# A hand-planned attention and MoE kernel: the same steps in another order, on other engines and in other buffers

## The chip, the cores and the metric

The kernel runs on one core of one Trainium2 chip. A core has five engines that run side by side, each from its own queue in the order in which the instructions were written: TensorE (PE in the profile, with its weight loads as PEld), VectorE (DVE), ScalarE (ACT), GpSimd (POOL) and SyncE (SP), which here mainly issues transfers. Sixteen DMA engines move the data. The metric is the time of one execution on the device in microseconds (us), lower is better.

## The reference

Four batches of eight heads, 768 positions of 64 numbers. Each position attends to itself and the 95 positions before it, and to the first 8 positions; a bias grows with the distance. The result, 3072 tokens of 512 numbers, goes through two matrix products with a SoLU and a layer norm between them.

```python
scores = scale * np.matmul(q, k.transpose(0, 1, 3, 2))
...
bias = -slopes[:, None, None] * dist[None, :, :]
scores = np.where(keep, scores + bias[None], -1000000000.0)
a = np.exp(scores - np.max(scores, axis=-1, keepdims=True))
a = a / (np.sum(a, axis=-1, keepdims=True) + 1e-09)
x = np.matmul(a, v)                    # to (B*S, H*D) by token
...
h = x @ w_in
e = np.exp(h - np.max(h, axis=-1, keepdims=True))
solu = h * e / (np.sum(e, axis=-1, keepdims=True) + 1e-09)
ln = (solu - mu) / np.sqrt(var + 1e-06) * g_ln
out = ln @ w_out
```

## The kernel before

The program is written in two passes. In the first, the function builds a list of 1094 *steps* by calls of `step`; each has a number (the count of the calls), the engines on which it may run, the buffers that it takes and a function that emits its instructions. In the second, `Plan.order` walks three written lists: ORDER gives the numbers of the steps in the order in which they are emitted, SLOTS the buffer of each pool that a step takes, ENGS the engine of each step that has a choice (casts, copies, factor products, squares, statistics, the issue of the last stores). Since each engine works in the order of emission, these lists are the whole schedule. Waits between engines are put in from the data and buffers that the instructions share. A fourth list, WARM, names places (position in ORDER, PSUM bank, count) at which filler matmuls on a constant tile are emitted, so that PE is busy while it would wait (L1233).

What the steps do, with the names used below:

- Loads. SyncE issues q and k by batch and pair of heads (four pairs, p0 to p3; L475 and L482), v by pair in two halves (L489), v's end rows (`vends`, L497) and its first 8 rows (`vglob`, L504), the four quarters of w_in (L615), of w_out (L625), and g (L578). From the ninth transfer on, each issue also waits until an earlier one has landed.
- Casts to 16 bits of x (q or k; `x32` to `x16`), of v and of w_in (`copy`, L264 on ACT, L266 on DVE, L268 on POOL). q and k are then turned: by PE (`turn_q`, `turn_k`, L735) and copied out of PSUM, except in batch 3, where a transfer turns them (L770).
- Attention, by batch: `scores` in two groups of six blocks for each pair (bias by PE in batch 0, L872; products L886), the exponential on ACT (L894), and in batches 1 to 3 a multiplication by the factor `fb` (`fac`, L903, DVE or POOL). The first 8 positions have their own small keys (`kg`, L521, POOL), `gscores` (L940, L946) and values (`vgz`, L513, POOL). By unit of 384 queries (unit 0 and unit 1): `sums` (L967, L976), their logarithm and split, `spread` (L1022), A·V in two parts (`av1`, `av2`, L1066 and L1056), and the product xT (L1091, DVE). A·V needs all casts of v of that batch that it reads, the end rows among them.
- The MoE part, by tile of 128 tokens (24 tiles, t0 to t23): `gemm1` (eight matmuls, L1125), `ef` (ACT, L1131), `u` (DVE, L1134), the sum of squares `sq` (ACT L1141 or DVE L1145), then u is turned, in tiles 0 to 4 by PE (`turn_u`, L1160), from tile 5 on by a transfer (`uturn`, L1150; four `uu` buffers hold u, six places of `late` the turned one), `gemm2` (L1206), scaling (`osb`, L1217 or L1220) and the store (L1224).
- Once: w_out is scaled by g in eight blocks (`gw`, L638, L641, L645), its `mean` is taken by PE (L652), and the blocks are centred (`centre`, L656, DVE). gemm2 needs that.
- The statistics of each group of three tiles (`stats`, L1180 to L1183) and the scale from them (L1187, L1189).

PSUM has eight banks, taken one at a time or two at a time (`big`, by scores and gemm1).

Of the kernel before, what the change touches and what calls it, by code (L numbers as in the profile page):

```python
# [29 lines left out]
FACT = {1, 2, 3}  # L30
SPLIT = False
ORDER = """
# [28 lines left out]
"""  # L61
SLOTS = """
# [10 lines left out]
"""  # L73
ENGS = """
# [4 lines left out]
"""  # L79
WARM = """  # L80
25:0:16 30:2:4 37:3:2 48:5:3 59:3:2 117:7:4 156:6:5
"""


# [1187 lines left out]
```

## Time and profile before

| what | us |
| --- | --- |
| median of 3 runs (154.2 to 154.55) | 154.37 |
| the profiled execution | 154.43 |
| its span, first to last instruction | 152.7 |
| PE, ACT, DVE, POOL busy in it | 144.4, 123.3, 116.7, 67.2 |
| PE filler matmuls (36) | 10.8 |

The engine rows of the profile give the busy time of each engine; a busy PE is not PE at its peak. A row of a timeline gives the start, the length, the engine with its line, the operation, the tiles written and read, and in brackets how long the engine stood idle before it and what ended that. SPq rows are SyncE issuing transfers.

### The profile page before, as it was taken

Reading aid. Unit: us, or ns where it says so; the run is one execution under the profiler, and the core shown is the slowest. Engines: PE = TensorE matmul, PEld = TensorE weight load, DVE = VectorE, ACT = ScalarE, POOL = GpSimd, SP = SyncE. Lnnn points to the kernel's source line nnn. Section 1 sums busy time; section 2 is a strip of 40 time slices with the busy share of each in tenths; the row PEclk is TensorE's granted clock in tenths of the full one; section 3 lists DMA queues with packets and bytes.
Section 4 is the critical chain, followed back from the end, with each engine's and each line's share of the span. In section 5 each row is a group of like instructions: output and inputs, shape, how many; then the busy total and the mean of one; then the engine's idle time right before and its main releaser. Section 6 shows DMA issues by size and latency. Waiting matters only on the chain.

```text
span 152.7 us, 4815 instructions
## 1 busy us (share of the span) xinstructions
PE 144.4 (95%) x1877; PEld 77.6 (51%) x1877; DVE 116.7 (76%) x241; ACT 123.3 (81%) x212; POOL 67.2 (44%) x188
## 2 busy tenths in 40 slices
PE   6979799999999999999999999989999999999991
PEld 2445557467655466744454645444445644444450
DVE  6729978799999997889899857289794884898200
ACT  3948999699999989899997896796875776884642
POOL 7675446548399849935921233755031000110000
PEclk9999999999999999999999999999999999999999
DMA  4999999999999899999999999998999975488743
GB/s 133 372 298 341 288 380 336 355 339 397 282 272 189 235 300 234 229 266 253 237 131 228 249 167 236 177 206 171 197 216 228 197 214 112 88 227 219 228 158 137
DMA packets 76431, 36.35 MB, mean 238 GB/s; under 512 B 65457, under 2 KB 71929, under 8 KB 76409
## 3 DMA queue, kind: packets, MB, share of 16 engines
q1 hardware_dynamic: 76120, 35.54, 96.3%
q10 hardware_dynamic: 288, 0.52, 0.9%
q8 instruction: 14, 0.23, 0.7%
q14 instruction: 9, 0.07, 0.1%
HBM read 23.15 MB, written 6.29 MB: 193 GB/s over the span
## 4 chain that ended last, share of the span: by engine, by line
PE 67%; DMA 8%; SPq 7%; DVE 7%; ACT 5%; issue 3%; POOL 0%; DVEq 0%; ACTq 0%
PE acc L1206 22%; PE acc L1125 21%; PE acc L1066 7%; DMA x<-in_q_dram 3%; SPq L489 3%; DMA late<-uu 3%; PE acc L735 3%; PE acc L886 3%; PE acc L967 3%; PE acc L1022 2%; DMA v<-in_v_dram 2%; DVE uu L1134 2%; ACT ef L1131 2%; SPq L475 1%; PE acc L1056 1%
## 5 line engine op out<-in xcount | busy, mean ns | idle before, releaser
L1125 PE MATMUL acc<-w_in_sb,xT 128*128 128x512 f16 x192 | 44.4, 379 | 0.0
L1206 PE MATMUL acc<-gw_out_sb,late 128*128 128x512 f16 (+1 forms) x200 | 44.3, 371 | 0.0
L1134 DVE SCALAR_TENSOR_TENSOR uu<-ef,acc 128x1024 f16<-128x1024 f16 x24 | 29.2, 1217 | 6.4 <-ACT ef L1131 5.7
L894 ACT ACTIVATE eb<-acc 128x896 f16<-128x896 f32 (+1 forms) x32 | 29.3, 962 | 2.0 <-PE acc L886 2.0
L1131 ACT ACTIVATE ef<-acc 128x1024 f16<-128x1024 f32 x24 | 24.8, 1035 | 5.9 <-PE acc L1125 5.9
L1206 PEld LDWEIGHTS <-late 128*128 128x128 f16 x200 | 18.9, 98 | 20.9 <-issue 0.7
L1125 PEld LDWEIGHTS <-xT 128*128 128x128 f16 x192 | 18.1, 98 | 21.4 <-issue 1.1
L268 POOL CAST x<-x 128x384 f16<-128x384 f32 (+1 forms) x32 | 19.0, 622 | 20.3 <-DMA x<-in_q_dram 6.1
L1091 DVE TENSOR_TENSOR xT<-acc,rr 128x384 f16<-128x384 f32 x32 | 16.4, 551 | 4.4 <-ACT rr L1031 2.9
L1066 PE MATMUL acc<-eb,v 64*64 64x160 f16 (+4 forms) x448 | 16.0, 221 | 0.6 <-POOL v L268 0.3
L1141 ACT ACTIVATE sqa<-uu 128x1024 f16<-128x1024 f16 x15 | 16.1, 1071 | 0.0
L1066 PEld LDWEIGHTS <-v 64*64 64x64 f16 x448 | 12.7, 106 | 4.5 <-issue 2.7
L1031 ACT ACTIVATE rr<-acc 128x768 f32<-128x768 f32 x16 | 12.6, 811 | 2.2 <-PE acc L1022 1.3
L903 DVE TENSOR_TENSOR eb<-eb,fb 128x896 f16<-128x896 f16 (+1 forms) x19 | 13.0, 710 | 0.9 <-ACT eb L894 0.9
L903 POOL TENSOR_TENSOR eb<-eb,fb 128x240 f16<-128x240 f16 (+1 forms) x20 | 12.8, 670 | 0.2 <-ACT eb L894 0.2
L268 POOL CAST v<-v 128x384 f16<-128x384 f32 (+3 forms) x21 | 9.7, 476 | 7.1 <-DMA v<-in_v_dram 7.0
L735 PE MATMUL acc<-ident,x 128*128 128x128 f16 x144 | 11.1, 220 | 1.2 <-ACT x L264 0.7
L1233 PE MATMUL acc<-busy 128*128 128x512 f16 x36 | 10.8, 439 | 1.5 <-DVE busy L550 1.5
L886 PE MATMUL acc<-qT,kT 64*64 64x160 f16 (+2 forms) x384 | 11.3, 227 | 0.3 <-ACT qT L264 0.3
L1145 DVE SCALAR_TENSOR_TENSOR sqv<-uu 128x1024 f16<-128x1024 f16 x9 | 11.0, 1219 | 0.1
L735 PEld LDWEIGHTS <-x 128*128 128x128 f16 x144 | 8.4, 98 | 4.9 <-ACT x L264 1.9
L1217 ACT ACTIVATE x<-acc,rstd 128x512 f32<-128x512 f32 (+1 forms) x9 | 5.8, 640 | 6.2 <-PE acc L1206 6.2
(120 smaller groups left out, 206.2 us busy)
## 6 DMA issues: line engine op xcount, KB each, us to landing
x<-in_q_dram SPq DMA_DIRECT2D x16, 384.0 KB, 5.9
x<-in_k_dram SPq DMA_DIRECT2D x16, 384.0 KB, 5.3
out_dram<-osb SPq DMA_DIRECT2D x12, 256.0 KB, 4.8
v<-in_v_dram SPq DMA_DIRECT2D x12, 192.0 KB, 4.8
out_dram<-x SPq DMA_DIRECT2D x9, 256.0 KB, 2.2
late<-in_moe_w_in_dram SPq DMA_DIRECT2D x4, 512.0 KB, 6.6
w_out<-in_moe_w_out_dram SPq DMA_DIRECT2D x4, 512.0 KB, 6.0
v<-in_v_dram SPq DMA_DIRECT2D x12, 160.0 KB, 4.4
```

The source lines that it names most:

```text
L268: nc.gpsimd.tensor_copy(out=out, in_=in_)
L735: nc.tensor.transpose(out=pt[:, ts(j, P)], in_=a[:, j, ts(pp, P)], identity=ident)
L886: nc.tensor.matmul(out=sc[o : o + 64, par, col : col + n], lhsT=kk[r, BLK * c : BLK * c + BLK], rhs=qq[r, g0 : g0 + n], start=fresh, stop= ...
L894: ex["fn"] = (lambda ex=ex, qk=qk, gw=gw: nc.scalar.activation(out=eb[at(qk, "eb")][:, :, 0:gw], in_=big(qk)[:, :, 0:gw], func=AF.Exp, sca ...
L903: (nc.gpsimd if fx["at"] == "POOL" else nc.vector).tensor_tensor(out=e[:, :, y], in0=e[:, :, y], in1=fb[:, p, :, y], op=ALU.mult)
L1066: nc.tensor.matmul(out=o_[64 * h : 64 * h + 64, gl : gl + m], lhsT=vv[r, v_at(vi, h, c), pair, :], rhs=view(eb[at(e_own[b, gi, pair], "eb" ...
L1091: nc.vector.tensor_tensor(out=xT[at(xt_own[b], "xT")][:, p, q0:q1], in0=one(av, d)[:, 0:w], in1=rr[at(re, "rr")][:, d, 0:w], op=ALU.mult)
L1125: nc.tensor.matmul(out=ph()[:, ts(fh, 512)], lhsT=xT[at(xt_own[b], "xT")][:, j, ts(t % NA, P)], rhs=w_in_sb[:, j, ts(fh, 512)], start=(j = ...
L1131: ex["fn"] = lambda g1=g1, t=t, ph=ph: nc.scalar.activation(out=ef[at(g1, "ef")], in_=ph(), func=AF.Exp, accum_out=s0[:, t : t + 1])
L1134: u["fn"] = lambda u=u, g1=g1, t=t, ph=ph: nc.vector.scalar_tensor_tensor(out=uu[at(u, "uu")], in0=ef[at(g1, "ef")], scalar=USC, in1=ph(), ...
L1141: nc.scalar.activation(out=sqs_["ACT"], in_=uu[at(u, "uu")], func=AF.Square, scale=float(D_FF) ** 0.5, accum_out=s2[:, t : t + 1])
L1206: nc.tensor.matmul(out=one(g2)[:, 0:wd], lhsT=uT[at(el_o, "uT")][:, c, :], rhs=gw_out_sb[:, c, sl_], start=(c == 0), stop=(c == NFC - 1))
```

## The change

The four lists are replaced. No step is added, removed or cut differently, and no other line is touched. ORDER names the same 736 steps; of those behind the first eight transfers all orders are free.

```diff
 ORDER = """
-126 86 12 11 271 2 13 17 16 10 15 66 14 18 0 20 73 36 3 75 7 1 4 88 68 69 89 22 53 55 56 90 8 70 38 79 81
...
+126 271 24 52 6 12 2 13 16 60 15 11 3 4 18 5 20 86 66 0 68 23 62 73 99 36 14 17 53 19 22 88 89 7 75 76 90
...
 SLOTS = """
-0 1 2 3 4 5 0 0 1 2 0 0 1 1 2 0 0 1 3 3 1 2 4 2 2 3 4 0 5 1 2 5 6 3 0 0 1 3 3 1 2 1 0 2 2 3 3 1 1 4 2 2 0
...
+4 0 2 1 3 5 1 0 6 5 0 1 4 0 1 3 2 1 2 4 6 3 0 5 6 2 2 1 3 4 3 3 1 2 4 2 1 3 2 1 0 0 3 0 2 11 3 0 2 0 1 1
...
 ENGS = """
-1 0 0 1 1 1 1 1 2 0 2 1 0 0 2 0 1 0 1 0 0 0 1 2 2 2 1 1 2 0 0 1 1 1 1 0 1 2 2 0 2 1 2 1 0 1 0 0 1 1 1 0 1
...
+1 1 2 1 0 0 2 1 1 1 1 0 0 1 1 0 1 0 1 0 0 0 1 2 2 1 0 0 1 0 0 2 0 2 2 0 2 2 1 0 0 0 2 0 1 0 1 2 1 1 0 0 0
...
 WARM = """
-25:0:16 30:2:4 37:3:2 48:5:3 59:3:2 117:7:4 156:6:5
+9:0:4 24:0:16 59:0:2 80:4:4 117:6:5 166:3:2
```

Read out by engine, the lists say this:

| place | before | after |
| --- | --- | --- |
| first transfers on SyncE | q2 k1 q1 vglob k0 vglob k2 vends (batch 0) | g q0 q2 k1 q1 q3 vglob k0 (batch 0) |
| last quarter of w_in, of w_out (place in SyncE's line) | 28th, 45th | 28th, 45th |
| first matmul steps behind the first fillers | turn_k p1, turn_q p2 | turn_q p2, turn_q p1 |
| fillers | 16, 4, 2, 3, 2, 4, 5 | 4, 16, 2, 4, 5, 2 |
| right ahead of the first gemm1 (t2) | 5 fillers | turn_k of batch 1, p1 |
| behind the mean, not ahead of it | | gscores of batch 1 unit 1, scores of batch 1 group 0 p2 |
| uturn of t6, t7 in SyncE's line | 101st, 103rd | 95th, 98th |
| v loads of batch 3 in SyncE's line | 83rd, 89th, 110th to 115th | 103rd, 107th, 109th to 116th (with a uturn and a store between) |
| turning of batch 3's q and k by SyncE | 86th to 108th | 82nd to 106th |
| ends of PE's line | gemm2 t22, t21, t13, t23 | gemm2 t18, t16, t22, t21, t23 |

POOL's line between the last block of w_out and the cast of the end rows of batch 1 reads, before: kg, kg, cast k (batch 2, p1), fac, fac, cast v, cast q (batch 2, p1), stats, cast v, cast of the end rows; behind it vgz and a cast of v. After: kg, kg, cast v, kg, cast k (batch 2, p1), fac, cast q (p0), cast k (p0), cast q (p1), stats, fac (batch 1, group 1, p2), vgz, cast v, cast v, cast of the end rows.

Engines of the steps that have a choice, before and after:

| step | before | after |
| --- | --- | --- |
| cast of k | POOL 10, DVE 2, ACT 4 | POOL 9, DVE 4, ACT 3 |
| cast of q | POOL 7, DVE 6, ACT 3 | POOL 12, DVE 4 |
| cast of v, of its end rows | POOL 12 + 2, DVE 4 + 2, ACT 4 | POOL 15 + 3, DVE 1 + 1, ACT 4 |
| copy of turned k, q from PSUM | ACT 8 + 5, DVE 4 + 7 | ACT 7 + 9, DVE 5 + 3 |
| cast of w_in | POOL 4, ACT 2, DVE 2 | POOL 2, ACT 2, DVE 4 |
| gw | DVE 5, POOL 2, ACT 1 | POOL 5, ACT 2, DVE 1 |
| fac | DVE 19, POOL 5 | DVE 16, POOL 8 |
| sq | ACT 15, DVE 9 | ACT 12, DVE 12 |
| stats | POOL 6, DVE 2 | POOL 3, DVE 5 |
| osb | ACT 15, DVE 10 | ACT 17, DVE 8 |
| tripling of the bias | DVE | POOL |
| issue of the last stores | SP 3, ACT 2 | SP 4, ACT 1 |

79 rows, old and new, of tables (ENGS, ORDER, SLOTS) are left out of this document.

## The prediction

> **What bounds the kernel now.** First the page's engine table and its slices, then the sums by stage over five stretches that I chose at the places where the work changes its kind.
>
> ```profile
> PE 144.4 (95%) x1877; PEld 77.6 (51%) x1877; DVE 116.7 (76%) x241; ACT 123.3 (81%) x212; POOL 67.2 (44%) x188
> ...
> PE   6979799999999999999999999989999999999991
> ```
> ```profile
> 0.00:27.00 27.00, 23.41 (x380) 13.42 (x381) 19.81 (x60) 22.04 (x34) 16.18 (x75) 1.00 1.00 307
> 27.00:43.00 16.00, 15.35 (x242) 9.59 (x244) 14.88 (x30) 14.74 (x27) 9.38 (x20) 1.00 1.06 339
> 43.00:95.00 52.00, 52.00 (x755) 28.23 (x758) 46.21 (x84) 47.88 (x85) 31.62 (x68) 1.00 1.12 230
> 95.00:117.00 22.00, 21.11 (x264) 10.00 (x253) 16.04 (x28) 17.19 (x28) 9.20 (x22) 1.00 1.02 198
> 117.00:150.00 33.00, 32.55 (x260) 16.37 (x256) 19.81 (x42) 21.39 (x41) 0.83 (x4) 1.00 0.72 182
> ```
>
> In the sums the columns are busy us of PE, PEld, DVE, ACT and POOL, then the granted clock, the DMA share and GB/s. TensorE is the bound: from 43 to 95 us it is busy 52.00 of 52.00. What an order of the same steps can win is PE's idle time alone, because the matmuls stay: 3.59 us before 27 us (and the fillers there), 0.65 us from 27 to 43, 0.89 us from 95 to 117. The 0.45 us of the last stretch lie behind the last matmul. The first two stretches are paced by transfers: DMA shares of 1.00 and 1.06 mean that the engines' queues are full.
>
> **The change part by part.** No instruction's work changes except by its engine, so I take it place by place. I read ORDER engine by engine and ask at each place which matmuls stand ahead of it.
>
> *The start, up to the first gemm1 (tile 2).* In both orders exactly the same matmul steps stand ahead of it, and SyncE issues the same 28 transfers up to the last quarter of w_in. This is what happens there now:
>
> ```profile
> 26.14 1.24 PE L1233 MATMUL acc<-busy 128*128 128x512 f16 x5
> ...
> 27.22 1.89 PE L1125 MATMUL acc<-w_in_sb,xT 128*128 128x512 f16 x8
> ```
> ```profile
> 26.23 0.61 POOL L268 CAST w_in_sb<-late 128x512 f16<-128x512 f32 x1 [0.26 <-DMA late<-in_moe_w_in_dram]
> ```
> ```profile
> 18.60 0.33 SPq L578 DMA_DIRECT2D g<-in_moe_g_ln_dram  x1
> ```
>
> The last w_in quarter lands at 26.23, its cast ends at 26.84, and the five fillers hold PE until 27.38, so gemm1 begins about 0.35 us later than the weights allow. The change takes these five away (33 fillers in place of 36, none right ahead of gemm1). But it puts the load of g, 0.33 us of SyncE, ahead of all others, and the full queues carry that delay on. Bounds: 0.35 us earlier to 0.6 us later (the delay and one more 0.3 us of casts that now stand behind the xT products on VectorE). I take 0: the next paragraph says why either would be absorbed.
>
> *The mean (eight matmuls, L652).* It needs all eight scaled blocks of w_out.
>
> ```profile
> L641 POOL TENSOR_TENSOR gw_out_sb<-w_out,g x4: 612/612/614, 32.5 to 36.7; 128x256 f16<-128x256 f32 x4
> L625 SPq DMA_DIRECT2D w_out<-in_moe_w_out_dram x4: 367/368/413, 26.2 to 33.4; - x4
> ...
> DMA to landing us min/median/max: 6.0/6.0/6.0
> ```
> ```profile
> 41.07 1.90 PE L652 MATMUL acc<-gw_out_sb,onesm 128*128 128x512 f16 x8
> ```
>
> The last w_out load is issued at 33.4 and lands 6.0 us later, at 39.4. It is SyncE's 45th transfer in both orders, with the same 44 ahead. The change scales its second block on POOL: two halves of 0.612, so 40.6 us, against 41.07 now. But two short steps that stand ahead of the mean now (a batch 1 scores step, a gscores step) come behind it, so 0.4 us of the win is work put off. Net 0. Cover: the 0.65 us of PE idle between 27 and 43; without it, a late start would show in full.
>
> *Batch 1's A·V product.* Here the change costs. It gives POOL the casts of batch 2's q0 and k0 (ACT's now) and puts the factor product of group 1, pair p2 ahead of the cast of the end rows of v, which A·V of batch 1, unit 0 needs. These are POOL's rows now, and PE's row of that A·V:
>
> ```profile
> 37.27 0.47 POOL L521 TENSOR_TENSOR kg<-kT,hpick 128x16 f16<-128x16 f16 x2
> 40.80 2.02 POOL L268 CAST x<-x 128x384 f16<-128x384 f32 x2 [3.06 <-PE acc L886]
> 42.78 4.82 POOL L903 TENSOR_TENSOR eb<-eb,fb 128x240 f16<-128x240 f16 x8
> 47.55 0.90 POOL L268 CAST v<-v 128x320 f16<-128x320 f32 x2
> 48.39 0.95 POOL L268 CAST x<-x 128x384 f16<-128x384 f32 x2
> 49.31 0.20 POOL L1180 TENSOR_TENSOR sq<-sums 128x6 f32<-128x6 f32 x1
> ...
> 50.21 1.00 POOL L268 CAST v<-v 128x320 f16<-128x320 f32 x2
> 51.15 0.72 POOL L268 CAST v<-vt 128x256 f16<-128x256 f32 x1
> 52.15 1.62 POOL L513 TENSOR_TENSOR vgz<-vgn,pick 128x256 f16<-128x256 f32 x2 [0.27 <-DMA vgn<-vgn]
> 54.07 0.96 POOL L268 CAST v<-v 128x320 f16<-128x320 f32 x2 [0.30 <-DMA v<-in_v_dram]
> 54.99 0.21 POOL L521 TENSOR_TENSOR kg<-kT,hpick 128x16 f16<-128x16 f16 x1
> ```
> ```profile
> 56.02 0.26 PE L1066 MATMUL acc<-eb,v 64*64 64x160 f16 x4
> ```
>
> Now the end rows are cast by 51.87 and A·V at 56.02 waits for nothing. After the change POOL does, between the last w_out block (40.6) and that cast's end: three kg steps 0.47 + 0.21, three v casts 0.90 + 1.00 + 0.96, four casts of x at 0.95, two factor products at 4.82 / 2 = 2.41, the statistics 0.90 (49.31 to 50.21), vgz 1.62, the end rows 0.72. That is 0.68 + 2.86 + 3.80 + 4.82 + 0.90 + 1.62 + 0.72 = 15.40 us, so 56.0: the very moment at which PE asks. The slack of 4 us is gone. What POOL waits now (0.27 and 0.30 us for transfers) or does slowly (the cast of 2.02 us in place of 0.95, 1.07 more) then falls on PE. Bounds: 0 and 15.40 + 0.57 + 1.07 + 0.9 (v's first cast cannot begin before its load, some 6 us behind w_out's as everywhere here) = 2.5 us. I take 0.4, near the lower end, because the long cast and the two waits all came of transfers and neighbours that are moved too, and one wait of 0.30 is what the nearest row shows to be usual.
>
> *The two holes from 95 to 117 us.* From the chain of waits, PE's timeline and SyncE's:
>
> ```profile
> 95.25 4.58 DMA late<-uu
> 99.95 1.23 DVE uu L1134 x2
> ...
> 111.83 3.06 DMA v<-in_v_dram
> ```
> ```profile
> 101.24 0.22 PE L872 MATMUL acc<-bw,identb 64*64 64x64 f16 x2 [0.56 <-DVE uu L1134]
> ...
> 115.51 0.25 PE L1066 MATMUL acc<-eb,v 64*64 64x160 f16 x1 [0.33 <-POOL v L268]
> ```
> ```profile
> 85.58 1.97 SPq L1150 DMA_TRANSPOSE late<-uu  x1
> 87.60 0.57 SPq L482 DMA_DIRECT2D x<-in_k_dram  x1
> 88.23 2.21 SPq L482 DMA_DIRECT2D x<-in_q_dram  x1
> 90.53 1.92 SPq L1224 DMA_DIRECT2D out_dram<-osb  x1
> 92.56 1.26 SPq L770 DMA_TRANSPOSE qT<-x  x1
> ...
> 95.25 1.26 SPq L1150 DMA_TRANSPOSE late<-uu  x1
> ...
> 107.30 5.15 SPq L489 DMA_DIRECT2D v<-in_v_dram  x6
> ```
>
> First hole: the turning of tile 6's u is issued at 95.25, behind two loads, a store and two other turnings; it lands 4.58 us later, only then is its uu buffer free, u of tile 13 runs, and the scores that need its PSUM wait 0.56 us. The change issues it right behind the turning of tile 8 (85.58 plus 1.97), so near 87.6, 7.7 us sooner. The hole closes: -0.56. Second hole: the six v loads of 107.30 to 112.45 come last in SyncE's line. The change puts all eight v loads of batch 3 and one more store there, some 1.7 us of issuing (two at 0.6 and 0.5); but SyncE stood still for about 1.6 + 1.4 us in the rows at 88.23 and 90.53, and batch 3's last k load moves ahead of that. The last v then comes about 1.3 us sooner, more than the 0.33 us: -0.33. Bounds of both together: 0 and -0.89.
>
> *The rest.* Three squares go from ACT to DVE, three factor products and three w_out blocks more to POOL, six casts net too; the tripling of the bias goes to POOL. Between 43 and 95 us DVE is busy 46.21 and ACT 47.88 of 52.00 us, POOL 31.62, so this is relief where it is tight; PE has no idle time there to win. The end (nine gemm2 in a row, then 3 us of scaling and store) is the same. 0.
>
> **Sum**, against the profiled execution of 154.43 us (span 152.7 and 1.73 around it; the median of the three runs is 154.37): 154.43 + 0 + 0 + 0.4 - 0.56 - 0.33 = 153.94, say 153.9.
>
> **The rivals.**
> *More than forecast.* POOL stays in time and the start keeps its 0.35 us: 154.43 - 0.35 - 0.89 = 153.2. For it: the fillers really are gone. Against: g's issue.
> *No change.* The holes come back elsewhere: the same twelve turnings of 1.3 us still pass one queue before the last v load, and POOL's wait of 0.4 us eats what is left. 154.4.
> *Slower: POOL becomes the bound of A·V in batch 1.* Place: the cast of the end rows. It decides once POOL's 15.40 us grow by more than the 0.9 us that the holes give back. Price up to 2.5 us: 154.43 + 2.5 - 0.89 = 156.0; at the middle of its range, 1.7, 155.2. Against: POOL never kept PE waiting between 43 and 95 us so far. For it: the sum has no slack, and the cast at 40.80 took twice the one at 48.39.
> The Trainium skill, in "SBUF — State Buffer", section "SBUF: two separate sides", says that VectorE and GpSimd share one port pair under an exclusive lock, so that one of the two stands still while the other has it. The doubled cast lies beside DVE work and agrees; by that rule the busier POOL would pay such a toll again, and the slower rival would be the outcome.
> *Slower at the start.* The 0.6 us are not absorbed and no hole closes: 155.0.
>
> **How the numbers follow.** The forecast 0.35, more than forecast 0.17, no change 0.16, POOL the bound 0.24, slow start 0.08. A measurement of this kernel tells 0.2%, about 0.3 us, from no change. The forecast lies 0.47 under the median, so a small part of it (0.05) counts as no change: faster 0.30 + 0.17 = 0.47, same 0.05 + 0.15 of the no-change case = 0.20, slower 0.01 + 0.24 + 0.08 = 0.33. The range leaves out half of the best case's tail and the dearest third of POOL's: 152.9 to 155.5. The forecast's own range is 153.5 to 154.2.
>
> **What would show it.** Right: no idle time of PE before the scores near 100 us; the turning of tile 6 issued before 90 us; gemm1 without fillers ahead, the mean between 40.5 and 41.2 us. Wrong: an idle row of PE that names POOL v near 56 us; a POOL row of 2 us for one cast; a mean later than 41.5, which would put the loss into the transfers of the start; PE idle before gemm2 at 117 to 150 us, where I expect none.

## The result: 2.6% slower

| | before | after |
| --- | --- | --- |
| median us (runs) | 154.28 (4) | 158.29 (4) |
| range us | 153.61 to 154.55 | 157.57 to 159.31 |
| the profiled execution, its span | 154.43, 152.7 | 158.11, 156.4 |

The ratio is 1.0259 with a 95% interval of 1.0212 to 1.0305: 4.0 us lost where 0.5 us was forecast as a gain. All ratios below are against the kernel before in the same series on the same chip; they go by the executions within some 1.5% of a kernel's fastest, so a median over all its executions may stand higher than its ratio says.

The engine rows and slices of the changed kernel's page (each digit a fortieth of the span, in tenths):

```profile
PE 145.7 (93%) x1874; PEld 78.1 (50%) x1874; DVE 118.3 (76%) x243; ACT 121.3 (78%) x207; POOL 85.3 (55%) x208
...
PE   6959999997999998999999999999979999999991
```

And the same five stretches as before (busy us of PE, PEld, DVE, ACT, POOL, then clock, DMA share, GB/s):

```profile
0.00:27.00 27.00, 22.84 (x339) 12.98 (x343) 18.47 (x53) 20.48 (x32) 17.30 (x76) 0.94 0.96 292
27.00:43.00 16.00, 14.53 (x260) 9.43 (x250) 14.80 (x28) 15.70 (x26) 11.43 (x25) 1.00 1.05 321
43.00:95.00 52.00, 51.33 (x717) 27.25 (x714) 45.19 (x85) 47.02 (x82) 45.49 (x83) 1.00 1.12 228
95.00:117.00 22.00, 20.95 (x247) 10.11 (x247) 15.35 (x30) 18.10 (x32) 7.77 (x18) 1.00 1.12 207
117.00:150.00 33.00, 32.80 (x302) 16.27 (x301) 23.70 (x50) 17.97 (x34) 3.33 (x9) 1.00 0.70 162
```

PE did the same work and idled more in each of the first four stretches: 4.16 against 3.59 us, 1.47 against 0.65, 0.67 against 0.00, 1.05 against 0.89. In the first one the difference hides in fillers and in a granted clock of 0.94. (The clock isn't the cause of the 4 us: the four executions took 158.11 and 158.46 us with a mean clock of 0.989 and 0.987, and 157.57 and 159.31 with 1.0. But it shifts rows of this one profile: from 12 to 14 us its clock was 0.50.) The sharper reading is by places where both orders have done exactly the same matmul steps, so that the difference of PE's times there is loss, between these two executions:

| PE has done the same steps up to | before us | after us | lost so far |
| --- | --- | --- | --- |
| first gemm1 begins (32 steps) | 27.22 | 28.89 | 1.67 |
| mean and its neighbours done (58) | 43.54 | 45.63 | 2.09 |
| sums of batch 1 unit 1 done (71) | 56.02 | 58.46 | 2.44 |
| first A·V of batch 1 done (76) | 57.62 | 60.59 | 2.97 |
| gemm1 of tile 13 done (128) | 97.06 | 100.06 | 3.00 |
| last-but-one scores of batch 3 done (136) | 105.86 | 108.63 | 2.77 |
| sums of batch 3 unit 0 and a gemm2 done (145) | 114.75 | 118.54 | 3.79 |
| all but the last gemm2 (174) | 147.64 | 151.35 | 3.70 |

So there are three places: the start (1.67), 30 to 60 us (1.30), and the attention of batch 3 (1.0, after 0.2 had been won back). The rows of PE at these places in the changed kernel, from its timeline, with the wait that ended last in brackets:

```profile
28.89 1.89 PE L1126 MATMUL acc<-w_in_sb,xT 128*128 128x512 f16 x8
...
42.44 1.90 PE L653 MATMUL acc<-gw_out_sb,onesm 128*128 128x512 f16 x8
...
59.28 0.26 PE L1067 MATMUL acc<-eb,v 64*64 64x160 f16 x3 [0.43 <-POOL v L269]
...
108.32 0.22 PE L873 MATMUL acc<-bw,identb 64*64 64x64 f16 x2 [0.22 <-DVE uu L1135]
...
116.72 1.89 PE L1207 MATMUL acc<-gw_out_sb,late 128*128 128x512 f16 x8 [0.83 <-DVE uu L1135]
119.57 0.25 PE L1067 MATMUL acc<-eb,v 64*64 64x160 f16 x1 [0.20 <-POOL v L269]
```

The first hole of before (0.56 us at 101 us) is gone, and 0.22, 0.83 and 0.20 us stand in place of 0.56 and 0.33. (A line L1126 here is L1125 before; in the experiments below it is L1123, since their lists are wrapped in fewer lines.)

### The profile page after: what moved, and what is told of

It is laid out like the page before. It is cut to its first block, busy times and chain, and to the rows that moved or that the text cites. A ratio compares the mean times of both kernels' runs of the same rounds, so it can differ in the third digit from the quotient of the medians.

```text
span 156.4 us, 4811 instructions
## 1 busy us (share of the span) xinstructions
PE 145.7 (93%) x1874; PEld 78.1 (50%) x1874; DVE 118.3 (76%) x243; ACT 121.3 (78%) x207; POOL 85.3 (55%) x208
## 4 chain that ended last, share of the span: by engine, by line
PE 55%; POOL 11%; DMA 9%; ACT 7%; DVE 7%; issue 5%; SPq 3%; POOLq 0%; ACTq 0%; DVEq 0%
PE acc L1207 19%; PE acc L1126 18%; PE acc L1067 6%; ACT eb L895 5%; DMA x<-in_k_dram 5%; POOL eb L904 5%; DMA v<-in_v_dram 4%; POOL v L269 4%; PE acc L887 2%; POOL x L269 2%; PE acc L736 2%; DVE xT L1092 2%; SPq L476 1%; PE acc L1023 1%; PE acc L1057 1%
## 5 line engine op out<-in xcount | busy, mean ns | idle before, releaser
L1126 PE MATMUL acc<-w_in_sb,xT 128*128 128x512 f16 x192 | 44.4, 379 | 0.0
L1126 PEld LDWEIGHTS <-xT 128*128 128x128 f16 x192 | 18.0, 98 | 20.6 <-issue 0.7
L269 POOL CAST x<-x 128x384 f16<-128x384 f32 (+1 forms) x40 | 20.5, 544 | 12.0 <-DMA qT<-x 4.2
L904 POOL TENSOR_TENSOR eb<-eb,fb 128x224 f16<-128x224 f16 (+1 forms) x32 | 23.1, 751 | 1.8 <-ACT eb L895 1.8
L269 POOL CAST v<-v 128x384 f16<-128x384 f32 (+3 forms) x27 | 14.2, 547 | 14.2 <-DMA v<-in_v_dram 14.2
L1146 DVE SCALAR_TENSOR_TENSOR sqv<-uu 128x1024 f16<-128x1024 f16 x12 | 15.5, 1294 | 0.1
L736 PE MATMUL acc<-ident,x 128*128 128x128 f16 x144 | 12.3, 230 | 2.9 <-DVE x L267 1.2
L1142 ACT ACTIVATE sqa<-uu 128x1024 f16<-128x1024 f16 x12 | 12.7, 1057 | 0.2 <-DVE uu L1135 0.2
L1181 POOL TENSOR_TENSOR sq<-sums 128x6 f32<-128x6 f32 x3 | 0.6, 197 | 22.4 <-DVE sq L1181 22.4
L904 DVE TENSOR_TENSOR eb<-eb,fb 128x960 f16<-128x960 f16 (+1 forms) x16 | 11.9, 776 | 1.1 <-ACT eb L895 1.1
L736 PEld LDWEIGHTS <-x 128*128 128x128 f16 x144 | 9.3, 102 | 6.0 <-POOL x L269 1.8
L1234 PE MATMUL acc<-busy 128*128 128x512 f16 x33 | 9.9, 447 | 1.6 <-DVE busy L551 1.5
```

What stands on the lines that cost most here:

```text
L269: nc.gpsimd.tensor_copy(out=out, in_=in_)
L736: nc.tensor.transpose(out=pt[:, ts(j, P)], in_=a[:, j, ts(pp, P)], identity=ident)
L904: (nc.gpsimd if fx["at"] == "POOL" else nc.vector).tensor_tensor(out=e[:, :, y], in0=e[:, :, y], in1=fb[:, p, :, y], op=ALU.mult)
L1126: nc.tensor.matmul(out=ph()[:, ts(fh, 512)], lhsT=xT[at(xt_own[b], "xT")][:, j, ts(t % NA, P)], rhs=w_in_sb[:, j, ts(fh, 512)], start=(j = ...
L1146: nc.vector.scalar_tensor_tensor(out=sqs_["DVE"], in0=uu[at(u, "uu")], scalar=float(D_FF), in1=uu[at(u, "uu")], op0=ALU.mult, op1=ALU.mult ...
```

## The experiments

The theory after the first look was START: the new first transfers delay the first gemm1, and nothing behind absorbs it. Its rivals were POOL (the busier GpSimd is late for A·V) and LATER or TAIL (the loss is made by what comes behind). The two orders have done the same 150 steps on all engines at the first gemm1, and the same 336 at 57 us, so they can be exchanged at these two seams.

One thing has to be known before single rows are compared. A profile is one execution, and kernels with the same orders up to the first gemm1 don't reach it at the same moment (us, from their timelines):

| start | runs | first exponential | first gemm1 |
| --- | --- | --- | --- |
| of before | before, s2_before_start, s2c_before_start, q2_swap_s2c, b2_t6_early, b3_cast_behind, m1_before_half | 13.28 to 14.35 | 26.72 to 27.67 |
| of before, g first | b1_g_first | 14.48 | 27.77 |
| changed | after, s3_after_start, s3c_after_start, m2_after_half | 14.18 to 15.12 | 27.95 to 28.89 |
| changed, g back | g1_back, f1_fac, q1_swap | 13.65 to 14.79 | 27.58 to 29.01 |
| changed, g ninth | g3_ninth | 13.64 | 27.57 |

On the mean the changed start has its first gemm1 1.4 us later (28.55 against 27.17); the 1.67 us of the table above come from one pair of executions.

**Exchange at the first gemm1: s2_before_start, s3_after_start.**

```diff
-steps up to gemm1 of t2 and the 28th transfer: orders, slots, engines of one kernel
+the same 150 steps: orders, slots, engines of the other kernel
```

> The orders, buffers and engines of the kernel before up to the first gemm1 (tile 2) and SyncE's first 28 transfers (150 of 736 steps, the same set in both kernels); everything behind them as in the changed kernel. Theory START (the changed first transfers put the first gemm1 1.7 us later, 28.89 against 27.22 us, and nothing behind absorbs it): 158.3 - 1.7 = 156.6 us, gemm1 of tile 2 at 27.2. Theory LATER (a late start is absorbed by the waits behind it; the loss is made by what comes after): 158.0 to 158.5 us, with gemm1 of tile 2 at 27.2 all the same.

> The counterpart: the changed orders, buffers and engines up to the first gemm1 and the first 28 transfers, everything behind them as in the kernel before. START: 154.3 + 1.7 = 156.0 us. LATER: 154.3 to 154.6 us.

Before's start with the changed rest: 1.0134 (1.0036 to 1.0232), median 156.38, as START had it. The changed start with the rest of before: 1.0215 (1.0093 to 1.0336), median 157.96, 2 us more than START had. Both had a wait of their own at the seam (PE there waited 1.5 and 2.1 us for a PSUM pair that the two parts number differently). Hence a second pair, in which the first part's buffers are renumbered.

**The same without the seam: s2c_before_start, s3c_after_start.**

> As s2_before_start, but the buffers of the first part are renumbered so that the second part finds free just the ones that it has in the changed kernel: the seam's own wait (1.6 us of idle PE before the spread of unit 1 in the profile) goes. START (the changed start is most of the loss): 156.4 - 1.6 = 154.8 us or less, 154.0 to 155.2. LATER (what comes behind the first gemm1 costs 2.4 us for itself, and the seam only hid in it): 156.0 to 156.6 us.

> The counterpart with the seam mended in the same way (2.3 us of PE waiting for a PSUM buffer there). START: 157.96 - 2.3 = 155.7 us, 1.7 over the kernel before; LATER: 154.0 to 154.6 us.

1.0147 (1.0084 to 1.021), median 157.38, and 1.017 (1.0109 to 1.0231), median 157.28. The seam's waits are gone from both profiles, and the first kernel didn't get faster by its ratio. The changed start costs some 1.7% even with the old rest. What the changed rest costs with the old start is less sure: the six executions of s2c_before_start took 155.17, 155.43 and 157.20 to 157.78 us, and 0.35 us of each lies outside the span (some 2.07 us around it, against 1.73 in the kernel before). The two ratios add up to 3.2% where the change costs 2.6; the intervals are too wide to say whether the parts hide each other. START is right, and whether it is enough stays open here.

**Engines without orders: e1_engs_before, e1b_order_before.**

```diff
 ORDER, SLOTS, WARM as they are
-ENGS of the same kernel
+ENGS of the other kernel
```

> The changed kernel with the engine choices of the kernel before (POOL gives back its three factor products, three w_out blocks and six casts), orders and buffers as changed. Theory POOL (the busier POOL, 85.3 against 67.2 us, and its waits on the way to A·V cost 1.8 us behind the mean): 156.5 us. Rival ORDER (the engines cost nothing by themselves; the loss lies in the order of transfers): 158.0 to 158.6 us. If the changed orders fit only the engines that they were made with, it is slower still, over 159 us.

> The kernel before with the engine choices of the changed one alone. POOL: 154.3 + 1.8 = 156.1 us or more, with idle PE that names POOL's v near 56 us. ORDER: 154.3 to 154.8 us.

188.27 us (1.2202, 1.2082 to 1.2321) and 172.17 us (1.1166, 1.1057 to 1.1274). These two say nothing about POOL as the bound. A step that goes to another engine lands in that engine's line at a place that was not made for it, and all behind it wait; the longest wait in e1b_order_before (us in total, times, longest) is one of the statistics, now early in GpSimd's line:

```profile
POOL sq L1178 <- DVE uu L1132: 24.3, 1, 24.3
```

Order and engines are one decision here.

**The load of g: g1_back, g2_issue, b1_g_first, g3_ninth.** The changed kernel issues g's 4 KB first of all, and its turning (PE) and evacuation (VectorE) stand early too. g1_back undoes all three; g2_issue leaves the load first and undoes the two others; g3_ninth puts the load behind the first eight; b1_g_first puts the load first in the kernel before.

```diff
 SyncE, g1_back
-g q0 q2 k1 q1 q3 vglob k0 vglob k2
+q0 q2 k1 q1 q3 vglob k0 vglob k2
...
-w_in(0) w_in(2)
+w_in(0) g w_in(2)
 SyncE, g3_ninth
-g q0 q2 k1 q1 q3 vglob k0 vglob k2
+q0 q2 k1 q1 q3 vglob k0 vglob g k2
 SyncE, b1_g_first
-q2 k1 q1 vglob k0
+g q2 k1 q1 vglob k0
 PE and VectorE, g1_back, g2_issue, g3_ninth
-turn_q p1, turn_g, turn_k p1
+turn_q p1, turn_k p1
...
-cast_q p3, evac_g, evac_q p0
+cast_q p3, evac_q p0
```

> The changed kernel with one thing of the start undone: the load of g, its turning on PE and the evacuation stand where they stood before (27th transfer, ahead of the first gemm1), so that the first load of a block of q is issued at 0.8 instead of 1.25 us. START BY g: 158.3 - 0.5 = 157.8 us or less, gemm1 of tile 2 at 28.3. START BY ORDER (the order of the other loads makes the late first landing, 8.28 against 5.24 us): no change, 158.0 to 158.6, first landing of k still over 7.5 us.

> The changed kernel with the turning of g (PE) and its evacuation (VectorE) back at their places behind the first attention unit, while its load stays the very first transfer. It splits what g1_back (156.2 us) undid. Theory ISSUE (the 0.45 us by which all loads are issued later, in a stream that never catches up): the gain of g1_back is gone, 157.8 to 158.6, gemm1 of tile 2 near 28.9. Theory ENGINES (the two little steps stand in the way of the first turnings and casts, on PE and VectorE): 156.0 to 156.6 us, gemm1 near 27.8.

> The kernel before with the load of g as the very first transfer and nothing else changed. ISSUE: all loads 0.45 us later, the first gemm1 0.5 later or more, time 154.6 + 0.5 to 154.6 + 1.0. ENGINES, or a delay that the waits behind absorb: within 0.2 us of the kernel before.

> The changed kernel with the load of g as the ninth transfer, behind the first eight loads instead of ahead of them; its turning and evacuation as in g1_back. If being FIRST costs (the 0.45 us of issue stand ahead of the first blocks of q and k): as g1_back, 1.009 to 1.015 of the kernel before. If being EARLY costs (one of the eight places in flight goes to 4 KB while the large loads wait for a place): 1.02 or more.

g1_back: 1.0113 (1.0056 to 1.0171), median 156.18; its interval lies wholly under that of the changed kernel. g2_issue: 1.0268 (1.0199 to 1.0338), median 158.96. So some 2 of the 4 us would hang on one load of 4 KB being first, and not on its two small steps: theory ISSUE. But three more kernels have g moved back (g3_ninth, and f1_fac and q1_swap below, with an edit each of their own), and one has it first (t1_triple below): over all, 1.0113 to 1.0185 without g first and 1.0187 to 1.0268 with it. So 1 to 2 us is a fair estimate. In the kernel before the same move costs 1.0057 (1.0019 to 1.0095), 0.9 us, with an interval of 0.3 to 1.5 us against its own 0.41 us. g3_ninth gave 1.0116 (1.0061 to 1.0172) with a median of 158.35 over all six executions; the ratio speaks for "being first", but with executions from 156.33 to 159.26 it is weak.

Where the delay goes is seen in the timelines of SyncE, ScalarE and PE. First before and b1_g_first:

```profile
0.78 0.46 SPq L475 DMA_DIRECT2D x<-in_q_dram  x1
...
13.95 0.92 ACT L894 ACTIVATE eb<-acc 128x896 f16<-128x896 f32 x1
```
```profile
0.78 0.41 SPq L576 DMA_DIRECT2D g<-in_moe_g_ln_dram  x1
1.25 0.43 SPq L473 DMA_DIRECT2D x<-in_q_dram  x1
...
14.48 0.92 ACT L892 ACTIVATE eb<-acc 128x896 f16<-128x896 f32 x1
...
27.77 1.89 PE L1123 MATMUL acc<-w_in_sb,xT 128*128 128x512 f16 x8
```

Then the changed kernel and g1_back:

```profile
0.79 0.40 SPq L579 DMA_DIRECT2D g<-in_moe_g_ln_dram  x1
1.25 0.93 SPq L476 DMA_DIRECT2D x<-in_q_dram  x2
...
15.12 5.14 ACT L895 ACTIVATE eb<-acc 128x896 f16<-128x896 f32 x6 [0.76 <-PE acc L887]
```
```profile
0.79 0.95 SPq L473 DMA_DIRECT2D x<-in_q_dram  x2
...
13.90 5.14 ACT L892 ACTIVATE eb<-acc 128x896 f16<-128x896 f32 x6 [0.16 <-PE acc L884]
...
27.83 1.89 PE L1123 MATMUL acc<-w_in_sb,xT 128*128 128x512 f16 x8
```

The first exponential is what the first loads lead to, and the first gemm1 follows it after 13.3 us (before: 27.22 - 13.95; b1_g_first: 27.77 - 14.48) or 13.8 to 13.9 us (after: 28.89 - 15.12; g1_back: 27.83 - 13.90). That holds in the other profiles too, however late the exponential came: 13.3 to 13.5 us in the eight with the start of before, 13.8 to 13.9 us in eight with the changed one. (The two exceptions are q1_swap with 14.2 us, and g2_issue with 15.9 us, where PE stood still for 1.7 us just before.) So the start is a chain of loads, casts, turnings, scores and six exponentials back to back, not a stream of transfers with room at its end.

How much of a shift is g's can't be read from these two pairs. The 0.5 us of b1_g_first against before lie within what the same start does from one execution to the next. And the 1.2 us between after and g1_back are in good part the clock of that one execution: from 10 to 15 us it was 0.66 in after and 1.00 in g1_back, and the two fillers ahead of the first scores took nearly twice as long, first in after and then in g1_back:

```profile
13.32 1.06 PE L1234 MATMUL acc<-busy 128*128 128x512 f16 x2
```
```profile
12.75 0.59 PE L1231 MATMUL acc<-busy 128*128 128x512 f16 x2
```

The same changed start at a clock of 1.00 in these 5 us began its first exponential at 14.18 (s3_after_start) and 15.03 (s3c_after_start), and q1_swap, without g first and at 1.00, at 14.79; there and in s3c_after_start VectorE's first cast waited for its load of q until 10.0, in g1_back it began at 9.41. What the load of g costs rests on the times above, not on these rows.

**The bias: t1_triple.**

```diff
 ENGS, step c_triple
-POOL
+DVE
```

> The changed kernel with the tripling of the bias back on VectorE, nothing else. If GpSimd's 1.24 us there hold up VectorE (a row of 2.83 us, 5.5 to 8.3, for an operation that took 0.41 us before), that row shrinks to about 0.4 us, VectorE's casts of q come up to 1.3 us earlier, and the time is 157.0 to 157.9. If the loads set the pace there: 158.0 to 158.6.

1.0187 (1.0118 to 1.0255), median 158.17. VectorE's row shrank from 2.83 to 1.63 us (not to 0.4), but its first cast of q began at 9.23 us in place of 9.40, since it then waited 0.56 us for its load. The interval overlaps that of the changed kernel, so no gain is shown; that the loads set the pace there agrees with this wait.

**The first hole: b2_t6_early, b3_cast_behind.** Both are the kernel before; the first makes the move on which the forecast's gain rested, and the second also exchanges two steps on VectorE.

```diff
 SyncE, both
-uturn t8, k(b3 p3), q(b3 p3), store t9, turn_q p2, turn_k p2, uturn t6
+uturn t8, uturn t6, k(b3 p3), q(b3 p3), store t9, turn_q p2, turn_k p2
 VectorE, b3_cast_behind
-cast_q b3 p3, u t13
+u t13, cast_q b3 p3
```

> The kernel before with one transfer moved: the turning of tile 6's u is issued right behind that of tile 8 (near 87.6 us, not 95.25). This is the step of the prediction that closes the first hole. Theory HOLE: PE's 0.56 us before the scores at 101 us go and are not given back: 0.3 to 0.6 us under the kernel before. Rival GIVEN BACK (the batch 3 transfers that it is put ahead of come 1.3 us later and open a hole of their own): within 0.2 us, or slower.

> As b2_t6_early, and on VectorE the cast of q of pair 3 (batch 3), which waits there 2.7 us for a buffer that the turnings free, goes behind u of tile 13, which had stood behind it. Theory SECOND CAUSE (the hole has two causes of nearly the same length, and only both together close it): PE's 0.6 to 0.8 us before the scores at 101 us go, time 0.4 to 0.8 us under b2_t6_early and 0.1 to 0.5 us under the kernel before. Rival: no change against b2_t6_early, with PE's wait at 101 us still there.

b2_t6_early: 1.0039 (1.0006 to 1.0072), median 155.11: no gain. Its VectorE and PE rows at the hole, and behind them those of VectorE in the kernel before:

```profile
99.48 0.82 DVE L264 CAST x<-x 128x768 f16<-128x768 f32 x1 [3.38 <-DMA kT<-x]
100.22 1.21 DVE L1132 SCALAR_TENSOR_TENSOR uu<-ef,acc 128x1024 f16<-128x1024 f16 x1
...
101.49 0.22 PE L870 MATMUL acc<-bw,identb 64*64 64x64 f16 x2 [0.77 <-DVE uu L1132]
```
```profile
98.74 0.80 DVE L266 CAST x<-x 128x768 f16<-128x768 f32 x1 [2.68 <-DMA kT<-x]
99.95 1.22 DVE L1134 SCALAR_TENSOR_TENSOR uu<-ef,acc 128x1024 f16<-128x1024 f16 x1 [0.41 <-DMA late<-uu]
```

u of tile 13 had waited only 0.41 us for the turning of tile 6. Ahead of it in VectorE's line stood a cast that itself had waited 2.68 us for a turning of k, and moving tile 6's turning ahead of those made it wait 3.38. b3_cast_behind: 0.9966 (0.9937 to 0.9996), median 154.48 against 155.18. There u goes as soon as its exponential is done, and PE runs on without a bracket:

```profile
99.41 1.22 DVE L1132 SCALAR_TENSOR_TENSOR uu<-ef,acc 128x1024 f16<-128x1024 f16 x1 [2.35 <-ACT ef L1129]
...
100.56 0.56 DVE L264 CAST x<-x 128x768 f16<-128x768 f32 x1
```
```profile
99.79 1.89 PE L1123 MATMUL acc<-w_in_sb,xT 128*128 128x512 f16 x8
101.61 0.22 PE L870 MATMUL acc<-bw,identb 64*64 64x64 f16 x2
```

The hole was worth some 0.5 us (0.1 to 1.0), about as forecast, but it took two edits. This kernel is the only one here with a ratio below 1, by a third of a per cent.

**The end of the attention of batch 3: f1_fac, q1_swap, q2_swap_s2c.**

```diff
 ENGS and VectorE, f1_fac (on g1_back)
-fac b3 g1 p1 on POOL, ahead of the last two casts of v
+fac b3 g1 p1 on DVE, behind fac b3 g0 p1
 SyncE, q1_swap (on g1_back), q2_swap_s2c (on s2c_before_start)
-uturn t8, uturn t6, turn_k(b3 p3), q(b3 p3)
+turn_k(b3 p3), q(b3 p3), uturn t8, uturn t6
```

> As g1_back, and one factor product of the last batch (group 1, pair 1; four instructions, 2.31 us on GpSimd, right ahead of the last casts of v) goes to VectorE, where 1.6 us are idle at that place. Theory POOL LATE (that product holds up the last casts of v, and so A·V of batch 3, which loses 0.78 us there): 0.5 to 0.8 us under g1_back. Rival TRANSFER (the last v loads land too late anyway, at 116.4): within 0.2 us of g1_back, and PE's wait there then names the same v.

> As g1_back, and in SyncE's queue the turning of tile 8's u (it stands there 3.57 us, 2.3 of them waiting for u) and that of tile 6 go behind the turning of k of pair 3 and the load of q of pair 3 of batch 3, which stood right behind them and were ready. Theory QUEUE (the wait delays every transfer behind it by 1.8 us, and these set the end of the attention of batch 3): tile 12's turning issued 1.5 us sooner or more, PE loses 1.2 us instead of 2.0 between 95 and 114 us, time 0.6 to 1.0 us under g1_back, 1.005 to 1.007 of the kernel before. Rival (SyncE waits elsewhere instead, or other things set that end): within 0.2 us of g1_back.

> As s2c_before_start (the orders before up to the first gemm1, the changed ones behind it), with the same swap in SyncE's queue. QUEUE: within 0.5% of the kernel before, with no run over 156. Rival: 1.012 to 1.018, as s2c_before_start.

f1_fac: 1.0143 (1.0087 to 1.0198), median 156.86, not under g1_back, and PE waits the same 0.2 us for the same v. Rows of the waits of PE by what they waited for, and of GpSimd's timeline, in f1_fac:

```profile
PE acc L1064 <- POOL v L266: 0.2, 1, 0.2
```
```profile
116.50 1.77 POOL L266 CAST v<-v 128x384 f16<-128x384 f32 x3 [1.93 <-DMA v<-in_v_dram]
```

GpSimd is free now and stands idle for the load: TRANSFER. q1_swap: 1.0185 (1.0139 to 1.023), median 158.44; q2_swap_s2c: 1.0123 (1.0064 to 1.0181), median 157.57. No gain either, and the reason is in the expectation, not in the rule: the turning of k that was put first was not ready. SyncE's waits between 78 and 122 us in q1_swap (us in total, times, longest) begin with

```profile
SPq L768 <- POOL x L266: 6.0, 2, 4.2
```

In g1_back the same wait is

```profile
SPq L768 <- POOL x L266: 2.3, 2, 1.8
```

so the swap put one wait in the place of another, for a cast of k on GpSimd. The two times don't compare well either: q1_swap's profiled execution began its first gemm1 at 29.01, 1.2 us after that of g1_back, with the same orders up to there. QUEUE was neither shown nor refuted.

**Exchange at 57 us: m1_before_half, m2_after_half.** At this seam the numbers of all eight PSUM banks and all other buffers could be made to agree.

```diff
-the first 336 steps (PE's 77, SyncE's 67 transfers): orders, slots, engines of one kernel
+the same 336 steps: orders, slots, engines of the other kernel
```

> The kernel before (orders, buffers, engines) for the first 336 of 736 steps, up to the A·V of batch 1 (PE's 77th step, SyncE's 67th transfer, some 57 us), and the changed kernel behind it. Theory TAIL (the transfers and casts of batch 3 in the changed order cost about 1.2 us between 95 and 125 us: there its profiles lose 3.3 us on the mean, the kernel before 2.3): 1.006 to 1.010 of the kernel before. Rival FIRST HALF (all of the loss is made ahead of 57 us; the lateness of SyncE's queue there is what shows up later): 0.998 to 1.003.

> The counterpart: the changed kernel for the first 336 steps, the kernel before behind them. TAIL: 1.015 to 1.020 of the kernel before, 1.2 us under the changed kernel. FIRST HALF: 1.022 to 1.030, as the changed kernel.

1.0058 (1.0026 to 1.0091), median 155.32, and 1.0124 (1.0066 to 1.0182), median 156.61. The changed first half costs 1.2%, 1.9 us (1.0 to 2.8), with the old second half behind it, less than both theories had. The changed second half costs some 0.6%, 0.9 us, behind the old first half, which is TAIL at the edge of its forecast. But the profile of m1_before_half shows a wait of 0.90 us right at the seam, which neither kernel of the study has. The changed order goes on with a turning of q, into a PSUM bank of the last `spread` of the first half. In the order of before that spread stands right ahead of it, and ScalarE hasn't read it yet:

```profile
57.59 0.81 ACT L1029 ACTIVATE rr<-acc 128x768 f32<-128x768 f32 x1 [1.08 <-PE acc L1020]
```
```profile
58.45 0.49 PE L733 MATMUL acc<-ident,x 128*128 128x128 f16 x6 [0.90 <-ACT rr L1029]
```

That wait is as long as the whole loss of this kernel. Between 95 and 117 us its PE idles 0.36 us where before idles 0.89: the old hole of 0.56 us is closed, and one wait is left there. GpSimd's rows show where it comes from:

```profile
116.36 0.25 PE L1064 MATMUL acc<-eb,v 64*64 64x160 f16 x1 [0.36 <-POOL v L266]
```
```profile
111.57 2.31 POOL L901 TENSOR_TENSOR eb<-eb,fb 128x224 f16<-128x224 f16 x4
113.83 2.47 POOL L266 CAST v<-v 128x320 f16<-128x320 f32 x4
```

So TAIL is not shown: without the seam's wait the kernel would stand near 1.000 by this one profile, inside the forecast of FIRST HALF. An exchange that is free of that wait was not run. FIRST HALF doesn't hold as it stands either, since m2_after_half lies under its 1.022. What the numbers allow is that the changed second half costs next to nothing behind an early first half, and some 1.3% behind the late one (2.6 less 1.2, with wide intervals); which wait makes that stays open.

## Why the prediction was wrong

**The start is the step that failed.** It was taken at 0, with bounds of -0.35 and +0.6, on the ground that "either would be absorbed". In the profiles of the changed start the first gemm1 came at 27.95 to 28.89, 0.7 to 1.7 us after the 27.22 of the prediction, so outside the bounds in each of them. It wasn't absorbed: s3c_after_start, which has only the changed start, is 1.7% slower than before (1.1 to 2.3), and m2_after_half, with the changed orders up to 57 us, 1.2% (0.7 to 1.8). Two things were wrong. The path was read as the transfers' (the last quarter of w_in, its cast, five fillers), while the first gemm1 follows the first exponential by 13.3 to 13.5 us however late that comes, and the changed order made that 13.8 to 13.9. And the cover named, 0.65 us of idle PE between 27 and 43, gave none: PE idles 1.47 us there in the changed kernel. Of the loss, 1 to 2 us hang on g being first in the changed order (g1_back, f1_fac, q1_swap and g3_ninth against after, g2_issue and t1_triple), and 0.9 us (0.3 to 1.5) in the old one; what else of the new start costs was not split further. The rival "slow start" had the place right and the price, 0.6 us, at a third.

**The mean** came at 42.44 us. The text had said that a mean later than 41.5 would put the loss into the transfers of the start; the place was right, and the start's chain, not its transfers alone, is what was late.

**A·V of batch 1.** Taken at 0.4. PE did wait 0.43 us for POOL's v at 59.28, the row that was named as the wrong sign. POOL's work between the last w_out block and the end rows of v took 16.47 us in place of the 15.40 worked out, as its rows say:

```profile
40.25 2.51 POOL L642 TENSOR_TENSOR gw_out_sb<-w_out,g 128x256 f16<-128x256 f32 x4 [1.87 <-DMA w_out<-in_moe_w_out_dram]
...
43.05 1.34 POOL L269 CAST v<-v 128x320 f16<-128x320 f32 x2
...
58.83 0.40 POOL L269 CAST v<-vt 128x256 f16<-128x256 f32 x1
```

from 42.76 to 59.23; 0.73 us of it is a wait, and the two halves of the cast at 43.05 took 1.34 us where 0.90 was counted. The chain began 2.2 us late, and PE came to this product 2.4 us late, so the size of the term, 0.4, was right. (The upper bound of 2.5 is 0.57 + 1.07 + 0.9 alone, on top of 56.0.) The rival "POOL becomes the bound" had the place and, by this row, a tenth of the loss; no run isolates GpSimd's part, since e1_engs_before and e1b_order_before fell apart elsewhere.

**First hole, -0.56.** The price was right (b3_cast_behind gains 0.5) and the reason half wrong: the chain named the turning of tile 6, which alone buys nothing (b2_t6_early). The hole is closed in the changed kernel, which also casts that q on GpSimd. The step meant to close it did not come as told: the turning of tile 6 was issued at 91.22, not near 87.6, because that of tile 8, ahead of it, held SyncE for 4.10 us in place of 1.97.

**Second hole, -0.33.** It failed. The last load of v was to come 1.3 us sooner; SyncE had issued it at 115.03, against 112.45 before, 2.6 us later in a kernel that was by then some 2.8 us late. The wait for v shrank from 0.33 to 0.20 only, a new one of 0.83 for u stands ahead of it, and in m1_before_half, with the early first half, the wait for v is 0.36. The text counted how soon SyncE would issue the last load of v, and not who else waits for that line: the turning of tile 14, which the change puts among those loads, frees the buffer that u of tile 17 takes. VectorE's row in the changed kernel:

```profile
115.44 1.22 DVE L1135 SCALAR_TENSOR_TENSOR uu<-ef,acc 128x1024 f16<-128x1024 f16 x1 [1.52 <-DMA late<-uu]
```

**The rest** (relief of ACT and VectorE is worth nothing between 43 and 95 us): held. From the first A·V of batch 1 to gemm1 of tile 13 the loss stays at 3.0 us. The direction was missed because of the start, and because the attention of batch 3 lost 1.0 us more behind it instead of winning 0.89. The first half alone accounts for 1.2 of the 2.6%; most of the rest shows only with both halves changed, and its cause stays open.

## What to carry to other kernels

Price a transfer that goes ahead of all others by the chain that hangs on the first load, not by its own issue: 0.4 us cost 0.9 us (0.3 to 1.5) in one order and 1 to 2 us in the other. Before a shift between two profiles is given a cause, look how far two executions of the same start lie apart: 27.58 and 29.01 us here. When a wait names its releaser, look at what stood ahead of the waiting instruction on its own engine and when that came free: removing the named cause buys only the difference (0.41 of 3.1 us here). And lists of orders, engines and buffers that were found together can't be taken over in part, except at a seam where both have done the same steps; and there the seam's own waits (1.5, 2.1 and 0.90 us here) have to be looked for before the parts are priced.

## What the runs showed of the hardware

A VectorE operation on 128x8 numbers took 2.83 us in the changed kernel and 0.41 in the one before. The rows of the changed kernel on VectorE and GpSimd, and then VectorE's in t1_triple:

```profile
5.47 2.83 DVE L382 SCALAR_TENSOR_TENSOR junk<-pick,rf 128x8 f32<-128x8 f32 x1
```
```profile
5.49 0.81 POOL L269 CAST x<-x 128x768 f16<-128x768 f32 x1
6.26 1.24 POOL L269 COPY bw<-bw 128x1280 f16<-128x1280 f16 x1
7.46 0.82 POOL L269 CAST x<-x 128x768 f16<-128x768 f32 x1
```
```profile
5.46 1.63 DVE L379 SCALAR_TENSOR_TENSOR junk<-pick,rf 128x8 f32<-128x8 f32 x1
```

It stood as long as GpSimd's three copies together (0.81 + 1.24 + 0.82 = 2.87 us), and with the tripling taken from GpSimd as long as the two casts (1.6). In g2_issue, where GpSimd waited 0.27 us for a load ahead of the third, it took 2.06 us, as long as the first two (0.81 + 1.25). GpSimd's operations, back to back, were not held up by it. The Trainium skill, in "SBUF — State Buffer", section "SBUF: two separate sides", says that the two engines share a port pair under an exclusive lock, held for the whole instruction. These rows agree with the lock; but by their lengths VectorE waited for two or three instructions in a row, until GpSimd's line had a gap. The toll falls on either side: here on VectorE, and on GpSimd, as the rival in the prediction had it, in the cast at 43.05 (1.34 us in place of 0.90), beside which VectorE ran a factor product of 0.65 us from 43.38 on. That VectorE's 2.83 us cost the kernel any time was not shown (t1_triple).
